# Attention, Fourier mixing and feed-forward on one core: seven block products in two more half batches, one exponential per score piece, and five PSUM banks in one ring

## The chip, the cores and the metric

The kernel runs on one core of a Trainium2 chip. A core has a matrix engine (TensorE, PE in the profile; its weight loads are the row PEld), a vector engine (VectorE, DVE), a scalar engine (ScalarE, ACT), a third one for elementwise work on SBUF (GpSimd, POOL) and a queue for transfers (SyncE, SP). Matrix products land in PSUM, which has eight banks of 128 x 512 fp32; DVE and ACT read them from there. The metric is the time of one execution on the device in microseconds, the median of several runs.

## What is computed

Eight batches of eight heads with 576 tokens and 64 dimensions each go through attention with a mask by blocks of 64. The heads are put together to 512 columns, mixed by a two-dimensional Fourier transform (the real part is added), and go through a normalisation and two layers with a relu between them:

```python
scores = scale * np.matmul(q, k.transpose(0, 1, 3, 2))
scores = np.where(block_i >= block_j, scores, -1000000000.0)
attn = np.exp(scores - np.max(scores, axis=-1, keepdims=True))
attn = attn / (np.sum(attn, axis=-1, keepdims=True) + 1e-09)
x = np.matmul(attn, v)                      # then 8 heads side by side: 576 x 512
X = np.fft.fft(np.fft.fft(x, axis=1), axis=2)
u = x + np.real(X)
un = (u - mu) / np.sqrt(var + 1e-06)
out = u + np.maximum(un @ w_ch1, 0.0) @ w_ch2   # 512 -> 2048 -> 512
```

## The kernel before, in words

All matrix products are made from fp16 pairs: a number is a high and a low half, and a product of two numbers is three matmuls (high by high, high by low, low by high).

**Attention** works head by head, 64 heads. For each head four pieces of scores are made for the row maxima (`max_part`, line 621), reduced by DVE into a tile `M`; `shift` (650) turns the maxima over on PE, ACT writes them to `mt`, and a transfer puts them into a row of the tile `lead`, so that the scores made next (`scores`, 680, four pieces too, from the tiles `rest` and `lead`) come out shifted already. ACT then takes the exponential of each piece twice from the PSUM bank, once into fp16 (`ph`) and once into fp32 (`p32`, shown as `p`), and POOL subtracts the two into the low half `pl`. `values` (708) multiplies them with the split values (`VH`, `VL`) into the bank `av`; DVE divides by the sums.

**The transform** of a batch (`fourier_steps`, 791) is folded and made in two stages on PE (`ps<-dft,fs` and `ps<-dft,zs` or `zc`). Of its second stage DVE makes `dif` and `add`, and POOL adds them to the tiles `X`, `U` and `u`, four operations for each of three pieces. What follows is the normalisation of 128 rows at a time (`norm`, 988: DVE statistics `st` and `ag`, a power on POOL, `un` on DVE), and `turn` (1002): PE turns it over, ACT and DVE split it into `uh` and `ul`.

**The feeds.** 256 rows at a time, a half batch, go through the two layers as one feed (`feed_steps`, 1036). There are 18 of them, and they are the bulk of PE's work. The first layer makes 16 blocks of 128 hidden columns (`h<-uh,W`, 256 columns per matmul); ACT and DVE split each pair of blocks into `gh` and `gl`; the second layer adds the products of these with the second weights (`acc<-W,gh`, 512 columns) into two banks `acc`. The feeds 15 to 17 (`SEVEN`, line 53) take the second layer by Strassen's seven products instead of eight (`seven`, 1135), 256 columns each, for each of 8 block pairs k: for this ACT writes the relu of the block in fp32 (`V`), POOL makes four sums of it (`x`, in `summed_up`, 1103), ACT and DVE split those (`ph`, `pl`). The sums of the weights (`combined`, 1405) are made after the last head, in the buffers that attention has left. Seven products need seven half banks for their sums: two `acc`, `av`, and one bank taken from `ps`.

**Order.** PE, DVE, ACT, POOL and SP each work strictly in the order in which the program was written. This order comes from a planner (1476 to 1532) that runs when the program is built: lanes of steps (attention, transform, weights) with assumed costs, and the feeds as filler between them. It books the assumed costs in a queue for each engine and gives PE the filler when no step of a lane is ready. Seven PSUM banks stand in three rings (`BANKS`, 51): `ps` three for attention and transform, `h` two for the first layer, `acc` two for the second; `av` has the eighth. Until the first feed begins all seven are lent to whoever asks; from then on steps get `ps` alone, and the feeds have `h` and `acc` to themselves.

## Time and profile before

| what | value |
|---|---|
| median of 3 runs | 1211.73 us (1210.74 to 1212.89) |
| profiled execution: time, span | 1207.94 us, 1206.1 us |
| TensorE clock granted, mean | 0.961 |
| busy, share of the span | PE 94%, PEld 70%, DVE 62%, ACT 50%, POOL 40% |
| instructions | PE 10338, DVE 1615, ACT 1338, POOL 630 |
| time of the DMA queues | q1 24.1%, q10 4.2%, q0 2.1% of 16 engines |

The profile is of one execution. It names tiles without their numbers, so `ps<-lead` stands for all maxima and half of the scores, `h<-uh,W` for the first layer, `acc<-W,gh` for the second. Nearly all instructions show the line 203, of a helper that keeps the order (229 and 232 for PE), so groups are told apart by tiles. A busy time of PE runs to the modelled end of each matmul; how fast matmuls follow each other is read from the starts.

### The profile page before, as it was taken

Reading aid. Unit: us, or ns where it says so; the run is one execution under the profiler, and the core shown is the slowest. Engines: PE = TensorE matmul, PEld = TensorE weight load, DVE = VectorE, ACT = ScalarE, POOL = GpSimd, SP = SyncE. Lnnn points to the kernel's source line nnn. Section 1 sums busy time; section 2 is a strip of 40 time slices with the busy share of each in tenths; the row PEclk is TensorE's granted clock in tenths of the full one; section 3 lists DMA queues with packets and bytes.
Section 4 is the critical chain, followed back from the end, with each engine's and each line's share of the span. In section 5 each row is a group of like instructions: output and inputs, shape, how many; then the busy total and the mean of one; then the engine's idle time right before and its main releaser. Section 6 shows DMA issues by size and latency. Waiting matters only on the chain.

```text
span 1206.1 us, 26181 instructions
## 1 busy us (share of the span) xinstructions
PE 1138.9 (94%) x10338; PEld 840.6 (70%) x10338; DVE 742.1 (62%) x1615; ACT 604.5 (50%) x1338; POOL 482.5 (40%) x630
## 2 busy tenths in 40 slices
PE   5767788999899999999999999999999999999998
PEld 4544475676677777777777777777677767788885
DVE  6877886666847673666647475757475657454421
ACT  5656667755565555536555346545554323233320
POOL 4552624534434434243442424353334333545420
PEclk9758789999799999999999999999999999999999
DMA  8785453333323342323325133413240010000000
GB/s 260 224 246 170 144 132 99 95 111 89 109 57 118 95 115 67 86 66 104 90 67 158 34 85 112 128 31 104 69 124 16 29 40 19 23 10 10 18 18 18
DMA packets 66128, 108.27 MB, mean 90 GB/s; under 512 B 9671, under 2 KB 36209, under 8 KB 66006
## 3 DMA queue, kind: packets, MB, share of 16 engines
q1 hardware_dynamic: 58662, 82.25, 24.1%
q10 hardware_dynamic: 4384, 16.78, 4.2%
q0 software_dynamic: 2960, 7.58, 2.1%
q8 instruction: 81, 1.33, 0.5%
q14 instruction: 41, 0.34, 0.1%
HBM read 58.50 MB, written 18.89 MB: 64 GB/s over the span
## 4 chain that ended last, share of the span: by engine, by line
PE 83%; DVE 5%; DMA 4%; POOL 3%; ACT 3%; issue 1%; SPq 0%; ACTq 0%; DVEq 0%; POOLq 0%
PE h L229 30%; PE acc L229 28%; PE ps L229 16%; PE av L229 8%; DMA lead<-mt 2%; DVE W L203 1%; POOL u L203 1%; PE ps L232 1%; DVE M L203 1%; POOL pl L203 1%; ACT p L203 1%; ACT ph L203 1%; ACT W L203 1%; DVE VL L203 1%; DMA lead<-rest 1%
## 5 line engine op out<-in xcount | busy, mean ns | idle before, releaser
L229 PE MATMUL h<-uh,W 128*128 128x256 f16 x2304 | 432.2, 274 | 0.2 <-DVE gl L203 0.2
L203 POOL TENSOR_TENSOR pl<-p,ph 128x288 f16<-128x288 f32 (+1 forms) x256 | 259.4, 1024 | 365.3 <-ACT p L203 337.0
L229 PEld LDWEIGHTS <-W 128*128 128x128 f16 x3456 | 332.7, 98 | 60.4 <-issue 1.3
L229 PE MATMUL h<-ul,W 128*128 128x256 f16 x1152 | 315.3, 274 | 0.0
L229 PE MATMUL acc<-W,gh 128*128 128x512 f16 (+1 forms) x1008 | 289.5, 370 | 0.0
L203 DVE TENSOR_REDUCE M<-ps 128x1 fp32r<-128x320 f32 (+3 forms) x293 | 131.3, 484 | 119.3 <-PE ps L229 118.8
L229 PE MATMUL acc<-W,gl 128*128 128x512 f16 (+1 forms) x504 | 186.2, 370 | 0.0
L229 PE MATMUL ps<-lead 73*128 73x288 f16 (+8 forms) x708 | 161.4, 291 | 15.4 <-DMA lead<-in_c_masks_dram 6.8
L203 ACT ACTIVATE ph<-ps 128x288 f16<-128x288 f32 (+1 forms) x235 | 119.5, 510 | 111.4 <-PE ps L229 110.6
L203 ACT ACTIVATE gh<-h 128x512 f16<-128x512 f32 x138 | 82.5, 598 | 166.6 <-PE h L229 161.6
L203 DVE SCALAR_TENSOR_TENSOR gl<-h,gh 128x512 f16<-128x512 f32 x138 | 94.7, 687 | 114.9 <-ACT gh L203 114.3
L229 PEld LDWEIGHTS <-ph 128*128 128x128 f16 x2112 | 133.1, 103 | 26.8 <-issue 4.6
L229 PEld LDWEIGHTS <-gh 128*128 128x128 f16 x1056 | 98.4, 99 | 67.8 <-issue 4.7
L229 PE MATMUL av<-VH,pl 128*128 128x65 f16 (+1 forms) x963 | 117.0, 201 | 8.4 <-POOL pl L203 6.5
L203 ACT ACTIVATE p<-ps 128x288 f32<-128x288 f32 (+1 forms) x235 | 119.0, 508 | 2.2 <-POOL pl L203 1.0
L229 PE MATMUL av<-VH,ph 128*128 128x65 f16 (+1 forms) x966 | 118.4, 203 | 0.7 <-ACT p L203 0.7
L229 PE MATMUL av<-VL,ph 128*128 128x64 f16 x960 | 116.7, 200 | 0.0
L229 PEld LDWEIGHTS <-pl 128*128 128x128 f16 x1056 | 103.5, 102 | 12.7 <-POOL pl L203 8.5
L229 PE MATMUL ps<-rest 128*128 128x320 f16 (+3 forms) x356 | 99.4, 292 | 1.0 <-DVE M L203 0.9
L229 PEld LDWEIGHTS <-lead 73*128 73x128 f16 (+1 forms) x744 | 66.7, 103 | 36.4 <-issue 8.1
L229 PEld LDWEIGHTS <-gl 128*128 128x128 f16 x528 | 51.5, 98 | 55.3 <-issue 0.5
L229 PEld LDWEIGHTS <-rest 128*128 128x128 f16 x372 | 38.8, 104 | 34.9 <-issue 15.3
(255 smaller groups left out, 1611.1 us busy)
## 6 DMA issues: line engine op xcount, KB each, us to landing
raw<-in_qk_dram SPq DMA_DIRECT2D x30, 576.0 KB
W<-in_moe_w_ch_dram ACTq DMA_DIRECT2D x14, 1024.0 KB
V<-in_v_dram SPq DMA_DIRECT2D x32, 320.0 KB
rest<-lead SPq DMA_DIRECT2D x64, 144.0 KB
rest<-rest SPq DMA_DIRECT2D x60, 144.0 KB
out_dram<-u SPq DMA_DIRECT2D x32, 256.0 KB
xd<-x SPq DMA_DIRECT2D x30, 256.0 KB
lead<-lead SPq DMA_DIRECT2D x60, 72.0 KB
```

The lines of the kernel that those rows point to most:

```text
L203: x = f(*args, **kw)
L229: return tc.keep_in_program_order(nc.tensor.matmul(*args, **kw))
L232: return tc.keep_in_program_order(nc.tensor.transpose(*args, **kw))
```

## The change

Five things are changed together.

1. `SEVEN` is 13 to 17 in place of 15 to 17: two more feeds take their second layer by seven products.
2. From head index 17 on (`ONCE`), `scores` takes one exponential per piece, into fp32, and ACT casts that copy to fp16 instead of reading the bank again. The bank is free after the first of the two.
3. Once feed 2 is done, the two `h` banks join the ring of `ps`: five banks, of which each step takes the one that has been free longest by the plan. A feed's first layer holds its bank from its first matmul to its last reader (`hold`, `drop`).
4. A new `pair_max` for two heads at once would begin at pair `GP`. `GP` is 32, and there are 32 pairs, so no step of it is ever made. What stays of it: four tiles `M` in place of two, six memsets of its constants on POOL at the very start, ahead of the transfers of the masks, three memsets of 64 columns, and split tiles that are shifted by 64 columns.
5. The planner leaves out single-bank steps that come later than a waiting step for two banks; there is no such step.

```diff
-SEVEN = range(15, 18)
+ONCE = 17
+SEVEN = range(13, 18)
+GP = 32
...
+    for i in range(2):
+        gpsimd.memset(MAIN[i], LEAST)
+        gpsimd.memset(MAIN[i][0:64, 0:1], 0.0)
+        gpsimd.memset(DIAG[i], LEAST)
     for i in range(HF):
         gpsimd.dma_start(LEAD[i][D:KS], c_masks)
...
+    def next_banks(n):
+        def first(x):
+            return (sorted(rings[x], key=lambda y: y[0]) if shared_out else rings[x])[:n]
+        return min(((x, first(x)) for x in lent if len(rings[x]) >= n), key=lambda x: max(y[0] for y in x[1]))
...
-        scalar.activation(ph[:, at:at + w], t[:, 0:w], AF.Exp, scale=0.125)
-        yield
+        if h < ONCE:
+            scalar.activation(ph[:, at:at + w], t[:, 0:w], AF.Exp, scale=0.125)
+            yield
         p32 = work.tile([P, 512], F32, name="p32", bufs=2)
         scalar.activation(p32[:, 0:w], t[:, 0:w], AF.Exp, scale=0.125)
         yield
+        if h >= ONCE:
+            scalar.copy(ph[:, at:at + w], p32[:, 0:w])
+            yield
         gpsimd.tensor_tensor(pl[:, at:at + w], p32[:, 0:w], ph[:, at:at + w], op=ALU.subtract)
...
     def max_lane():
-        for h in range(B * H):
+        for h in range(2 * GP):
...
+        for g in range(GP, B * H // 2):
+            for n in range(4):
+                yield Step(lambda n=n: pair_max(g, n), ...)
...
             if f % 2 == 0 and part == 0:
-                gs[f] = ps["h"].tile([P, 512], F32, name="h")
+                gs[f] = ps_tile() if me > 2 else own_tile()
...
     while True:
+        if not shared_out and ("F", 2) in done:
+            shared_out.append(True)
+            rings["ps"] += rings.pop("h")
```

The planner's inputs change, so the order changes on every engine. On PE the first 1744 matmuls are alike in the two orders; the one after them starts at 263.7 us of the trace; on DVE, ACT and POOL (but for the memsets) they part at about the same place. From there attention runs further ahead: in the new order the last head's values stand at a place with 107 us less PE work before it.

First place, the exponentials, on ACT: pieces 3 and 4 of one head, which `ps_3913` and its neighbour hold (`p` is the fp32 copy, `bs` the transform's). Before:

```order
L203 ACTIVATE ph_3911<-ps_3913 128x512
L203 ACTIVATE p_3967<-ps_3913 128x512
L203 ACTIVATE ph_3933<-ps_3935 128x512
L203 ACTIVATE p_3988<-ps_3935 128x512
L203 COPY bs<-ps_3977 128x258
```

The same place on ACT in the new order:

```order
L211 ACTIVATE p_3974<-ps_3913 128x512
L211 CAST ph_3911<-p_3974 128x512
L211 ACTIVATE p_3993<-ps_3928 128x512
L211 CAST ph_3926<-p_3993 128x512
L211 COPY bs<-h_3986 128x258
```

The count stays the same; `ph` comes second now, and only one instruction of each pair reads the bank.

Second place, DVE between the two normalised halves (`un`) of feed 3 and their split (`ul`), at 311 to 317 us of the trace of before. `M` rows are attention's maxima, `vacc` and `pw` a scale of attention. Before:

```order
L203 TENSOR_SCALAR un_4190<-u_3220,ag_4151 128x512
L203 TENSOR_SCALAR un_4204<-u_3220,ag_4171 128x512
L203 TENSOR_REDUCE M_0_94<-ps0_4181 128x1
L203 TENSOR_REDUCE M_0_94<-ps1_4194 128x1
L203 COPY vacc_4126<-ps0_4230 128x3
L203 TENSOR_SCALAR pw_4234<-vacc_4126 128x2
L203 SCALAR_TENSOR_TENSOR vacc_4126<-pw_4234 128x1 x2
L203 TENSOR_SCALAR pw_4234<-vacc_4126 128x1
L203 TENSOR_SCALAR vacc_4126<-pw_4234 128x1
L203 TENSOR_TENSOR ul_4254<-ps1_4255,uh_4253 128x4x128
L203 TENSOR_TENSOR ul_4254<-ps2_4261,uh_4253 128x4x128
```

The same place on DVE now:

```order
L211 TENSOR_SCALAR un_4241<-u_3238,ag_4197 128x512
L211 TENSOR_REDUCE M_2_99<-ps1_4191 128x1
L211 TENSOR_REDUCE M_2_99<-h0_4193 128x1
L211 TENSOR_REDUCE M_2_99<-ps0_4243 128x1
L211 TENSOR_SCALAR M_2_99<-M_2_99 128x1
L211 TENSOR_SCALAR un_4320<-u_3238,ag_4204 128x512
L211 TENSOR_SCALAR DEN_0_105<-av_4213,vacc_3294 128x5
L211 RECIPROCAL rec_4334<-DEN_0_105 128x5
L211 TENSOR_TENSOR x_4332<-av_4213,rec_4334 128x5x64
L211 TENSOR_TENSOR ul_4255<-ps1_4256,uh_4254 128x4x128
L211 COPY vacc_4154<-ps2_4325 128x3
```

Maxima and one head's division stand between the two halves now, and the second `ul` follows nine rows below the last of these.

Third place, POOL where the last batch's transform meets the feeds by seven products. `X`, `U` and `u<-u,dif` or `add` with 257 or 255 columns are the transform's, `x` the sums of seven products. Before, at 1038 to 1045 us, in feed 15:

```order
L203 TENSOR_TENSOR X_14755<-X_14755,dif 33x257
L203 TENSOR_TENSOR X_14755<-X_14755,add 33x255
L203 TENSOR_TENSOR U_14754<-U_14754,add 32x257
L203 TENSOR_TENSOR U_14754<-U_14754,dif 32x255
L203 TENSOR_TENSOR x<-V 128x128 x2
L203 TENSOR_TENSOR x<-x,V 128x128
L203 TENSOR_TENSOR x<-V,x 128x128
L203 TENSOR_TENSOR u<-u,dif 128x257
L203 TENSOR_TENSOR u<-u,add 128x255
```

And on POOL now, between the feeds 14 and 15 (the first two rows are the end of feed 14):

```order
L211 TENSOR_TENSOR u<-u,dif 128x256
L211 TENSOR_TENSOR u<-u,add 128x256 x2
L211 TENSOR_TENSOR X_15044<-X_15044,dif 33x257
L211 TENSOR_TENSOR X_15044<-X_15044,add 33x255
L211 TENSOR_TENSOR U_15043<-U_15043,add 32x257
L211 TENSOR_TENSOR U_15043<-U_15043,dif 32x255
L211 TENSOR_TENSOR u<-u,dif 128x257
L211 TENSOR_TENSOR u<-u,add 128x255
L211 TENSOR_TENSOR u<-u,add 128x257
L211 TENSOR_TENSOR u<-u,dif 128x255
L211 TENSOR_TENSOR x<-V 128x128 x2
L211 TENSOR_TENSOR x<-x,V 128x128
```

The sums for the first block pair of a feed by seven products stand behind ten rows of the transform and of the feed before, where they stood behind four. The transform of the batch before that one now meets the start of feed 13 in the same way; before, it met attention.

More of the change, by code (lines that the diff above doesn't have):

```diff
@@ L160 @@
     key: object = None
-    bank: bool = False
+    bank: int = 0
+    hold: object = None
+    drop: object = None
     need: tuple = ()
@@ L280, in split @@
         if g == GF:
-            return tuple(stage[i].rearrange("p c d -> p (c d)").bitcast(F16)[:, 0:2 * S] for i in range(2))
+            return tuple(stage[i].rearrange("p c d -> p (c d)").bitcast(F16)[:, 0:(64, 0)[i] + 2 * S] for i in range(2))
         return half_tiles(g % 2)[2:4]
-    M = [const.tile([P, 6], F32R, name=f"M_{i}") for i in range(2)]
+    M = [const.tile([P, 6], F32R, name=f"M_{i}") for i in range(4)]
+    MAIN, DIAG = ([const.tile([P, 5], F32, name=f"{x}_{i}") for i in range(2)] for x in ("MAIN", "DIAG"))
     DEN = [const.tile([P, 5], F32, name=f"DEN_{i}") for i in range(2)]
@@ L320, in ready @@
         if step.bank:
-            return max(r, min(rings[x][0] for x in lent))
+            return max(r, *(x[0] for x in next_banks(step.bank)[1]))
         if step.place > H and not step.cost:
@@ L357, in issue @@
                 x.forget(now)
-        free = None
+        free = []
         starts = []
@@ L378, in issue @@
         if step.bank:
-            current = min(lent, key=lambda x: rings[x][0])
-            rings[current] = rings[current][1:] + [t if free is None else free]
+            ring, got = next_banks(step.bank)
+            rings[ring] = [x for x in rings[ring] if not any(x is y for y in got)] + got
+            for n, x in enumerate(got):
+                x[0] = float("inf") if step.hold else free[min(n, len(free) - 1)] if free else t
+            if step.hold:
+                held[step.hold] = got[0]
+            given[:] = got
+        if step.drop in held:
+            held.pop(step.drop)[0] = t
         parts = step.emit()
@@ L1191, in both_steps @@
                     after = (("t", me, 0), ("t", me, 1)) + ((("g", me, k - 2),) if k > 1 else ())
-                yield Step(lambda part=part: both(k, part), 0.654, (), after, ("h", me, k) if last else None)
+                yield Step(
+                    lambda part=part: both(k, part), 0.654, (), after, ("h", me, k) if last else None, 0 if part else 1,
+                    hold=None if part else ("h", me, k),
+                )
         def split_steps(k):
@@ L1211, in feed_steps @@
             if not seventh:
-                seventh.append(turned.pop(0))
-                taken.append(rings["ps"].pop(0))
+                one = min(rings["ps"], key=lambda x: x[0])
+                rings["ps"] = [x for x in rings["ps"] if x is not one]
+                seventh.append(one[1:])
             nk = NF // 2
@@ L1485, in tile_attn_fourier_ffn @@
         ]
+        claim = min((heads[i].place for i in able if heads[i].bank == 2 and max(done[x] for x in heads[i].after) <= now), default=None)
+        if claim is not None:
+            able = [i for i in able if heads[i].bank != 1 or heads[i].place <= claim]
         until = [ready(heads[i]) for i in able] + ([ready(filler)] if filler is not None and may(filler) else [])
@@ L1525, in tile_attn_fourier_ffn @@
             if len(lent) > 1:
-                now = max(now, ready(filler), *rings["h"], *rings["acc"])
+                now = max(now, ready(filler), *(x[0] for x in rings["h"] + rings["acc"]))
                 lent = ["ps"]
```

95 lines of the change are left out of this document (68 added, 27 removed).

## The prediction

> **What bounds the kernel now.** I read the page first, for the engine that is busy and for when it is not.
>
> ```profile
> span 1206.1 us, 26181 instructions
> PE 1138.9 (94%) x10338; PEld 840.6 (70%) x10338; DVE 742.1 (62%) x1615; ACT 604.5 (50%) x1338; POOL 482.5 (40%) x630
> PE   5767788999899999999999999999999999999998
> PEclk9758789999799999999999999999999999999999
> ```
>
> PE is the only engine near its limit, and its gaps lie in the first quarter. The stretches of the trace say where exactly (columns: length, busy time of PE, PEld, DVE, ACT and POOL with instructions, clock granted, DMA share, GB/s).
>
> ```profile
> 0.00:264.00 264.00, 209.62 (x1747) 145.31 (x1748) 199.81 (x422) 174.48 (x383) 119.24 (x136) 0.85 0.56 169
> 264.00:292.00 28.00, 28.00 (x266) 20.23 (x265) 16.41 (x38) 15.46 (x39) 8.39 (x9) 1.00 0.06 17
> 292.00:318.00 26.00, 19.02 (x179) 14.23 (x178) 22.45 (x53) 13.93 (x34) 16.29 (x23) 0.74 0.60 170
> 318.00:400.00 82.00, 82.00 (x855) 60.02 (x853) 53.33 (x119) 47.56 (x110) 33.60 (x38) 1.00 0.28 83
> 400.00:700.00 300.00, 300.00 (x2875) 220.59 (x2873) 180.05 (x429) 150.11 (x343) 119.39 (x148) 1.00 0.32 88
> 700.00:1040.00 340.00, 340.00 (x3060) 246.32 (x3059) 207.34 (x449) 153.41 (x347) 125.58 (x152) 1.00 0.24 68
> 1040.00:1060.00 20.00, 18.36 (x166) 16.12 (x165) 11.96 (x25) 7.42 (x15) 16.90 (x33) 1.00 0.03 7
> 1060.00:1080.00 20.00, 20.00 (x186) 17.99 (x184) 6.49 (x11) 6.74 (x12) 6.94 (x16) 1.00 0.01 1
> ```
>
> Four stages follow. Up to 264 us PE waits a good deal, but its order there is not changed. From 292 to 318 us it idles 7 of 26 us: feed 2 is over, feed 3 waits for the transform of its batch, and DVE is busy 22.45 of 26. From 318 to 1040 us PE never rests, at full clock: only fewer or shorter matmuls can shorten this. At 1040 to 1060 it loses 1.64 us where the last transform meets feed 15. So the change can win by PE work, and win or lose at 292 and wherever a transform meets seven products.
>
> **The seven products.** The chain that ended last shows a feed with the plain second layer, per pair of blocks:
>
> ```profile
> 949.30 2.59 PE acc L229 x12
> 951.89 2.62 PE h L229 x24
> 954.51 2.59 PE acc L229 x12
> ```
>
> and, as further lines of that chain, one with seven products:
>
> ```profile
> 1060.35 2.62 PE h L229 x24
> 1062.96 0.66 PE acc L229 x6
> ...
> 1065.26 2.62 PE h L229 x24
> ```
>
> A plain pair takes 954.51 - 949.30 = 5.21 us, of which 12 matmuls of 512 columns are 2.59, 216 ns each. With seven products it is 1065.26 - 1060.35 = 4.91: 21 matmuls of 256 columns in 2.29 us, 109 ns each, about half as long for half the columns. The gain is 0.30 us a pair, 2.4 a feed with 8 pairs, **-4.8 us** for two feeds, all of it on PE where nothing hides it. The 16 pairs bring ACT, POOL and DVE work; beside a steady feed of that kind PE has 20.00 busy of 20 (row 1060:1080), so it is hidden there. The Trainium skill, "TensorE: Matmul & The Clock Gate", section "Back-to-back issue gap", gives a lower sustained spacing for streams with weight loads, about 131 ns at 512 columns and 81 at 128. An estimate by that page, with 98 ns between them for 256 columns, would be 96 x 131 = 12.6 us against 168 x 98 = 16.5, a loss of 3.9 us a feed. The rows above speak against it: 216 and 109 ns.
>
> **The start.** Six memsets now stand on POOL ahead of the masks' transfers, and the chain that ended last runs through these transfers:
>
> ```profile
> 2.06 4.65 DMA lead<-in_c_masks_dram
> ```
>
> POOL's timeline has memsets of this kind:
>
> ```profile
> 0.25 0.10 POOL L1561 MEMSET const-float32-0.0<- 128x1 f32 x1 [0.25 <-issue]
> 0.28 0.10 POOL L1561 MEMSET const-float32-1.0<- 128x1 f32 x1
> ```
>
> They follow each other by 0.03 us and take 0.10 each, so six delay the masks by 0.2 to 0.6 us, with nothing above them to hide it; a wait further on that is not for the masks may still swallow part. I take **+0.2**, the value by spacing. The three other memsets stand behind the work that frees their tiles, 0.1 us on an idle POOL: nothing.
>
> **One exponential.** Groups by form at 320 to 940 us (instructions, busy time, mean ns, idle time before):
>
> ```profile
> L203 ACT ACTIVATE ph<-ps 128x512 f16<-128x512 f32 x84 | 50.7, 605 | 19.9 <-PE ps L229 19.3
> L203 ACT ACTIVATE p<-ps 128x512 f32<-128x512 f32 x84 | 50.4, 602 | 0.8 <-POOL pl L203 0.6
> ```
>
> and the nearest row to a cast from SBUF, from the groups at 1030 to 1206 us:
>
> ```profile
> L203 ACT CAST ph<-x 128x512 f16<-128x512 f32 x24 | 14.8, 618 | 37.5 <-POOL x L203 37.5
> ```
>
> 618 ns against 605: ACT pays 0.01 us a piece, with half its time idle. `pl` waits for the second of the two in either order, `values` for `pl`, and the bank is free 0.6 us earlier. Priced alone, at 318 to 1040 us, where PE is full, it is **0**; a bank that frees earlier is worth something only where PE waits for banks.
>
> **Five banks, and attention ahead.** From 318 us on, PE is full before; the new order is worth nothing there unless it brings waits. Counted from the orders with the trace's spacing, the least PE work between a head's `shift` and its first scores is 4.0 us now and 4.3 before, and between a head's scores and its `values` 4.2 and 3.6. So the covers are of one size, and I take **+0.4** for the tighter transfers, between 0 and 3. The maxima, casts and DVE work of a head come 20% more densely while attention runs, which DVE at 180 of 300 us can carry.
>
> **The stage at 292 us.** What PE waits for there:
>
> ```profile
> PE ps L229 <- DVE M L203: 3.5, 3, 2.3
> ```
>
> and DVE's groups in this stage:
>
> ```profile
> L203 DVE TENSOR_REDUCE M<-ps 128x2 fp32r<-128x128 f32 (+4 forms) x14 | 6.0, 467 | 1.1 <-PE ps L229 1.1
> L203 DVE BATCH_NORM_STATS2 st<-u 128x6 f32<-128x512 f32 x3 | 2.0, 675 | 0.0
> L203 DVE TENSOR_TENSOR dif<-ps,bs 128x258 f32<-128x258 f32 (+1 forms) x3 | 1.3, 418 | 0.6 <-POOL U L203 0.6
> L203 DVE TENSOR_TENSOR x<-av,rec 128x320 f32<-128x320 f32 x1 | 0.5, 492 | 0.0
> ```
>
> Feed 3 begins when DVE has made its second `ul`. From the end of feed 2 to there, DVE's new order has three more maxima (3 x 0.467 = 1.4), one more division of a head (0.5 for `x`, 0.4 for its two small ones) and one more statistics (0.7 and 0.2 for the small row), and one `dif` and `add` less (0.8): about 2.4 us more on the engine that is busy 22.45 of 26. In return PE has done more by then: 14.0 us of work in place of 12.8 stand in the stage, and 2.1 us more before it. So feed 3 starts up to 2.4 us later with 3.3 us more done: **-0.9**. If DVE's extra falls into its 3.5 idle us, it is -3.3; if the low clock (0.74) also slows the 3.3 us of extra work to half speed, +2.4.
>
> **Transforms that meet seven products.** How it goes before: POOL's timeline has the transform's sums,
>
> ```profile
> 1042.77 1.41 POOL L203 TENSOR_TENSOR u<-u,add 128x255 f32<-128x255 f32 x2
> 1046.09 1.86 POOL L203 TENSOR_TENSOR u<-u,add 128x255 f32<-128x255 f32 x2
> ```
>
> and PE's waits of that time are
>
> ```profile
> 1047.42 0.28 PE L229 MATMUL av<-raw,pl 128*128 128x256 f16 x1 [0.89 <-DVE pl L203]
> ...
> 1053.47 0.66 PE L232 MATMUL ps<-ident,un 128*128 128x128 f32 x4 [0.74 <-DVE un L203]
> ```
>
> The sums `x` of seven products stand behind the transform's on POOL, then ACT and DVE split them, then PE gets them: 0.89 + 0.74 = 1.63 us, the idle time of 1040:1060. The transform of batch 6, hidden in attention before, now meets the start of feed 13 with the same rows on POOL: **+1.6**. The last transform stands between the feeds 14 and 15, with three sums of feed 14 ahead of it (0.7 us each by the rows above) and 5.6 us of PE work from its last matmul to the turn of feed 15, where 7.5 stood; in return that turn no longer waits for the last four `u`, 2.8 us. These about cancel: **+0.4**, between -1 and +3.
>
> **The sum.** -4.8 + 0.2 + 0 + 0.4 - 0.9 + 1.6 + 0.4 = -3.1 us, against the profiled execution's 1207.94 us (span 1206.1 and 1.84 around it): 1204.8. The median of the runs shown, 1211.73, is 3.8 above that execution; the terms are differences, so I take them from the median: **1208.6**.
>
> **Rivals.** A measurement of this kernel tells 0.2%, 2.4 us, from no change.
>
> *Waits eat the gain.* If both meetings cost 3 us each instead of 2.0 together, and the stage at 292 gives nothing: -4.8 + 0.2 + 0.4 + 6 = +1.8 at most, -0.5 with half of that; 1211.2. For it: PE has less work to put in between now that attention is over early. Against: after 1060 us the same feeds run without a gap. Chance 0.25.
>
> *The stage at 292 closes.* With five banks for attention, PE may make maxima and scores while DVE is late, and keep its clock: of the 7 us idle, 5 go: -4.8 + 0.2 + 2 - 5 = -7.6, 1204.1. Against: the row of waits names DVE, not banks. Chance 0.10.
>
> *The stage at 292 grows, and it ends slower.* DVE is the bound there. If the nine rows between the two `ul` wait for PE, whose matmuls stand behind a wait for DVE, the two go in turns, at the low clock. Feed 3 then starts 10 us later than I take it (the stage once more, by its 7 us of idle time and 3 at half speed): -3.1 + 10 = +6.9, 1218.6; from 5.5 us on it ends slower. Against: PE has 14 us of work there. Chance 0.10.
>
> *DVE and POOL lock each other out.* One `pl<-x,ph` on DVE's timeline shows 1.19 us while POOL's 1.86 above ran; the mean of its group at 1030 to 1206 us, below it, is 0.713:
>
> ```profile
> 1046.17 1.19 DVE L203 TENSOR_TENSOR pl<-x,ph 128x512 f16<-128x512 f32 x1
> ```
>
> ```profile
> L203 DVE TENSOR_TENSOR pl<-x,ph 128x512 f16<-128x512 f32 x24 | 17.1, 713 | 29.1 <-ACT ph L203 29.1
> ```
>
> With 16 more such instructions, each late by 0.48 us and none hidden, 7.7 us come on top: +4.6, 1216.3. Against: the mean says that most are not late, and the row 1060:1080 that PE does not see it. Chance 0.05. The Trainium skill, "SBUF — State Buffer", section "Who interferes with whom", says that a DVE instruction with two SBUF inputs and a POOL instruction that reads SBUF exclude each other for their whole length, which is this mechanism; the 1.19 us agrees.
>
> *The change does not do what it says.* For two heads' maxima at once this is certain (no step is made); for the rest the order shows it done.
>
> **How the numbers follow.** The forecast has 0.50, from 1204.5 to 1209.3. Faster by over 0.2%: 0.50 + 0.10 = 0.60, less 0.03 for its upper edge, 0.57. Same: 0.25 + 0.03 = 0.28. Slower: 0.10 + 0.05 = 0.15. The range goes from 1203 (the stage closes) to 1214 (all meetings at their upper bounds).
>
> **What would show it.** PE's last work should come 3 us earlier, the feeds 13 and 14 should have groups of 21 between those of 24, and 318 to 860 us should have no gap. A wait of PE for DVE `pl` or `un` should show at the start of the feeds 13 and 15, 1 to 3 us in sum each. The stretch from feed 2 to feed 3 should be 26 to 29 us long. I am wrong if that stretch is under 20 or over 35, or if PE has gaps while attention runs beside the feeds.

## The result, and the profile after

The changed kernel takes 1215.63 us (median of 11 runs, 1213.91 to 1222.28), the kernel before 1208.17 beside it (11 runs, 1207.33 to 1212.89): a ratio of 1.0063 with a 95% interval of 1.0045 to 1.0080. It is slower by 5 to 10 us; forecast was 3.1 us faster, and the range ended at 1214.0. The forecast of 1208.6 us was counted from a median of 1211.73 for before, 3.6 above the 1208.17 beside this result, so the two times lie only 7.0 us apart where the differences lie 10.6 apart. The profiled execution of it took 1219.95 us, 12.0 more than that of before and 4.3 more than its own median, so terms read from it are at the high end. Single executions that took over 1.5% longer than the fastest of their kernel (one of after_two_exp, one of cover_four_late, one of before in a later group) are left out of all ratios and medians below.

From the page after, the span, the totals and the two rows of PE in 40 slices:

```profile
span 1218.2 us, 26794 instructions
PE 1138.9 (93%) x10482; PEld 855.1 (70%) x10482; DVE 762.6 (63%) x1643; ACT 641.4 (53%) x1372; POOL 521.2 (43%) x709
PE   5667788999799999999999999999999999999998
PEclk9757789999799999999999999999999999999999
```

At this grain the two profiles can hardly be told apart. So I cut both at marks of the program: the last matmul up to which the orders agree (number 1744), the first of feed 3, of feed 13 and of feed 16. These are the first three stretches after that common part, of before (length, then busy time of PE, PEld, DVE, ACT, POOL with instructions, clock, DMA share, GB/s):

```profile
263.70:317.90 54.20, 47.22 (x447) 34.65 (x445) 38.76 (x90) 29.59 (x71) 24.78 (x32) 0.87 0.32 91
317.90:941.20 623.30, 623.30 (x6047) 456.26 (x6046) 380.98 (x886) 321.97 (x741) 248.09 (x304) 1.00 0.30 85
941.20:1080.40 139.20, 137.56 (x1091) 105.24 (x1090) 78.69 (x145) 43.63 (x87) 54.41 (x83) 1.00 0.07 24
```

and the same of after:

```profile
266.40:325.80 59.40, 50.25 (x504) 36.63 (x502) 43.75 (x99) 35.99 (x81) 29.02 (x38) 0.89 0.30 84
325.80:950.50 624.70, 619.42 (x5999) 451.19 (x5999) 402.68 (x916) 344.14 (x748) 258.38 (x303) 1.00 0.30 85
950.50:1092.60 142.10, 138.39 (x1224) 122.74 (x1223) 71.84 (x134) 52.24 (x102) 76.51 (x148) 0.99 0.07 23
```

The middle row of each is the news: 623.30 busy of 623.30 before, 619.42 of 624.70 after. The stretch that "never rests" now rests 5.28 us. The first stretch idles 9.15 us in place of 6.98, the last 3.71 in place of 1.64.

Idle time leaves out what a wait costs besides: matmuls that start again at a low clock, and short gaps that the tail of the matmul before covers. So in what follows I use **lost time**: the time from the start of one matmul to the start of another, less the spacing that each matmul between them has where PE is full (the median from start to start for its form, from 350 us of the trace of before on: 109 ns at 256 columns, 216 at 512). The sum of the spacings is PE's pure work: 1124.8 us before, 1119.9 after. In us, by stretch:

| kernel | PE work | to matmul 1744 | to feed 3 | feed 3 to 13 | feeds 13 to 15 | rest |
|---|---|---|---|---|---|---|
| before | 1124.8 | 55.4 | 13.2 | -1.0 | 2.2 | 0.6 |
| after | 1119.9 | 57.6 | 15.1 | 6.6 | 7.1 | 0.3 |

(A loss below zero is a few matmuls that follow each other faster than the median.) The first matmul starts 0.46 us later (below). 0.46 + 2.2 + 1.9 + 7.6 + 4.9 - 0.3 - 4.9 = 11.9: the 12.0 us are accounted for. What remains is to find which of it comes from what.

**The attention stage.** What PE waits for from 325 to 935 us, a list that is empty for the same stretch of before:

```profile
PE acc L244 <- DVE gl L211: 1.1, 1, 1.1
PE ps L244 <- DVE M L211: 1.1, 2, 0.7
PE ps L244 <- DMA lead<-rest: 0.9, 1, 0.9
PE ps L244 <- DVE vacc L211: 0.8, 1, 0.8
...
PE ps L244 <- ACT p L211: 0.3, 1, 0.3
```

No large wait, but a handful of small ones on DVE, ACT and transfers. In lost time, ten matmuls from feed 3 to feed 13 start over 0.25 us later than their spacing has it, 6.9 us in sum. Five of them (3.2 us) follow a read by DVE or ACT that has nothing to do with their operands, so I take it that they wait for the bank; three of these (1.7 us) are first layers of feeds. Three (2.9 us) wait for something of their own: the maxima, the transfer `lead<-rest`, and a feed's second layer for its own `gl` (1.3 us). For two (0.8 us) the trace names no reason. One of the first kind, on PE's timeline:

```profile
543.58 0.27 PE L244 MATMUL ps<-uh,W 128*128 128x256 f16 x1 [0.68 <-DVE M L211]
```

and on DVE's:

```profile
541.45 0.68 DVE L211 BATCH_NORM_STATS2 st<-left 128x6 f32<-128x512 f32 x1
542.16 0.18 DVE L211 BATCH_NORM_AGGREGATE ag<-st 128x2 f32<-128x6 f32 x1
542.26 0.67 DVE L211 BATCH_NORM_STATS2 st<-left 128x6 f32<-128x512 f32 x1
542.97 0.18 DVE L211 BATCH_NORM_AGGREGATE ag<-st 128x2 f32<-128x6 f32 x1
543.07 0.99 DVE L211 TENSOR_REDUCE M<-ps 128x1 fp32r<-128x320 f32 x2
```

`ps<-uh,W` is the feed, the work that PE always has in hand. Its bank belonged before to the feeds alone; now it comes from attention, whose maximum is still to be read by DVE, and DVE has the statistics of a row block in front of it. The work that was to hide attention's waits has in part become one that waits.

**Where transforms meet seven products.** The chain that ended last, at the start of feed 13, and PE's and POOL's timelines between the feeds 14 and 15:

```profile
958.24 1.24 POOL x L211 x3
960.02 2.75 POOL u L211 x4
963.55 0.60 DVE gl L211
964.15 1.11 DVE pl L211
965.59 0.66 PE acc L244 x6
```

```profile
1046.99 0.28 PE L244 MATMUL h<-dft,ZT 128*128 128x258 f32 x1
1049.09 1.11 PE L244 MATMUL h<-dft,zs 128*128 128x258 f32 x6 [1.82 <-ACT bs L211]
```

```profile
1046.69 1.41 POOL L211 TENSOR_TENSOR u<-u,add 128x256 f32<-128x256 f32 x2 [0.38 <-DVE u L211]
1048.06 0.72 POOL L211 TENSOR_TENSOR X<-X,dif 33x257 f32<-33x257 f32 x1
1048.74 0.72 POOL L211 TENSOR_TENSOR X<-X,add 33x255 f32<-33x255 f32 x1
```

The first is as forecast: the sums `x` of the products and the transform's `u` take turns on POOL, and feed 13 loses 1.39 us (0.07 before). The second is one step back: `bs` of the transform waits on ACT for DVE's `add`, `add` for POOL, and PE stands still in the middle of the transform. The feeds 14 and 15 lose 0.82 and 4.91 us (0.02 and 2.12 before).

**The products themselves** do what was forecast. Pairs of feed 13 on the chain that ended last:

```profile
977.50 2.62 PE ps L244 x24
980.12 0.66 PE acc L244 x6
...
982.41 2.62 PE ps L244 x24
```

982.41 - 977.50 = 4.91 us a pair, where a plain pair takes 5.21.

### The profile page after: what moved, and what is told of

It is laid out like the page before. It is cut to its first block, busy times and chain, and to the rows that moved or that the text cites. A ratio compares the mean times of both kernels' runs of the same rounds, so it can differ in the third digit from the quotient of the medians.

```text
span 1218.2 us, 26794 instructions
## 1 busy us (share of the span) xinstructions
PE 1138.9 (93%) x10482; PEld 855.1 (70%) x10482; DVE 762.6 (63%) x1643; ACT 641.4 (53%) x1372; POOL 521.2 (43%) x709
## 4 chain that ended last, share of the span: by engine, by line
PE 76%; DVE 8%; POOL 5%; DMA 5%; issue 3%; ACT 3%; SPq 1%; ACTq 0%; DVEq 0%; POOLq 0%
PE ps L244 25%; PE acc L244 25%; PE h L244 17%; PE av L244 8%; DMA lead<-mt 2%; POOL u L211 2%; DVE W L211 2%; DVE M L211 1%; POOL pl L211 1%; DMA lead<-rest 1%; PE ps L247 1%; DMA u<-in_moe_w_ch_dram 1%; SPq L211 1%; POOL U L211 1%; POOL X L211 0%
## 5 line engine op out<-in xcount | busy, mean ns | idle before, releaser
L244 PE MATMUL ps<-uh,W 128*128 128x256 f16 x1296 | 240.1, 274 | 1.4 <-DVE M L211 0.7
L244 PE MATMUL h<-uh,W 128*128 128x256 f16 x1008 | 187.7, 277 | 0.4 <-DVE vacc L211 0.2
L244 PE MATMUL ps<-ul,W 128*128 128x256 f16 x648 | 177.1, 273 | 0.0
L244 PE MATMUL h<-ul,W 128*128 128x256 f16 x504 | 139.4, 277 | 0.0
L244 PE MATMUL ps<-lead 73*128 73x288 f16 (+11 forms) x463 | 111.0, 300 | 20.0 <-DMA lead<-in_c_masks_dram 7.3
L211 DVE TENSOR_REDUCE M<-ps 128x1 fp32r<-128x192 f32 (+4 forms) x187 | 85.5, 491 | 49.7 <-PE ps L244 49.5
L211 ACT ACTIVATE p<-ps 128x288 f32<-128x288 f32 (+1 forms) x161 | 80.4, 500 | 40.3 <-PE ps L244 34.3
L211 ACT CAST ph<-p 128x512 f16<-128x512 f32 (+1 forms) x188 | 98.3, 523 | 5.1
L211 ACT ACTIVATE gh<-ps 128x512 f16<-128x512 f32 x81 | 48.0, 593 | 86.3 <-PE ps L244 83.5
L211 DVE SCALAR_TENSOR_TENSOR gl<-ps,gh 128x512 f16<-128x512 f32 x81 | 55.5, 685 | 55.7 <-ACT gh L211 55.0
```

Source lines behind the costliest of these rows:

```text
L211: x = f(*args, **kw)
L244: return tc.keep_in_program_order(nc.tensor.matmul(*args, **kw))
```

## The experiments

The theory after this comparison: PE's work did fall by 4.9 us, and three losses ate it: attention put further ahead with shared banks (about 7.6 us in the profiled pair), transforms beside seven products (4.9), and the stage at 292 us (1.9). The rivals: the cast is behind the attention stage's loss; the memsets are behind the later start; the crowded order is harmless and only the meetings cost. Beside the first four kernels, before took 1209.09 us (23 runs), beside the next four 1209.06 (29). Each group of kernels ran on another chip beside runs of before, so kernels of different groups are compared by their ratios to it.

### One part at a time

Three kernels make one part each, one takes the memsets from the changed kernel.

`seven_alone`, from before:

```diff
-SEVEN = range(15, 18)
+SEVEN = range(13, 18)
```

> The kernel before with one edit: seven products also in the feeds 13 and 14 (SEVEN from 13). Its order is that of before up to those feeds, and only the last transform meets them. Theory 'crowded order' (shared banks and attention pulled ahead cost the time, the feeds' gain is real): PE has 4.8 us less work, the last meeting costs about 1 us more; 1208.2 - 4.8 + 1 = 1204.4, ratio 0.997. Theory 'meeting' (the waits where transform and seven products meet eat the gain): 1208 to 1210, ratio 1.000 or above, with 4 us or more of new PE gaps between 940 and 1110 us.

1238.05 us, a ratio of 1.0242 (1.0223 to 1.0261): neither theory had 29 us. The stretch of the feeds 13 to 15, the wait in it, and what ACT makes there:

```profile
943.80:1110.00 166.20, 139.72 (x1234) 121.03 (x1233) 100.06 (x173) 62.93 (x120) 93.44 (x153) 0.95 0.07 20
```

```profile
967.69 0.37 PE L229 MATMUL ps<-raw,gh 128*128 128x256 f16 x1 [10.82 <-ACT raw L203]
```

```profile
966.10 0.62 ACT L203 CAST raw<-p 128x512 f16<-128x512 f32 x1 [2.75 <-DVE p L203]
```

`raw` here is no raw input any more. The second layer's summed weights are put into the tiles that attention leaves, and are made after its last head:

```python
            yield Step(
                lambda: combined(k), 0.0, ("X3.1", "A1.25", "G2.35"),
                (("V", B * H - 1, 4),) + ((("TT", k - 1),) if k else ()), ("TT", k),
            )
```

They take DVE, ACT and POOL from 966 to 1013 us here (46.7), and from 864 to 937 in the changed kernel (73). With attention's last head at 869 us of PE work and feed 13 at 867 there is no time for them, and feed 13 waits for one pair of weights after the other. I had not seen this in the forecast: the two more feeds of seven products can only be had because the shared banks pull attention ahead (its last head stands at 765 us of PE work in the changed kernel). The parts of this change aren't independent.

`once_alone`, from before:

```diff
+ONCE = 17
...
-        scalar.activation(ph[:, at:at + w], t[:, 0:w], AF.Exp, scale=0.125)
-        yield
+        if h < ONCE:
+            scalar.activation(ph[:, at:at + w], t[:, 0:w], AF.Exp, scale=0.125)
+            yield
...
+        if h >= ONCE:
+            scalar.copy(ph[:, at:at + w], p32[:, 0:w])
+            yield
...
```

The planner's list of assumed costs for a piece is changed to match.

> The kernel before with the one exponential per piece from head 17 on, nothing else. Theory 'crowded order' and theory 'meeting': 1208 +- 2, ratio within 0.998 to 1.002. Theory 'cast' (the cast holds ph, pl and the buffer of p longer, and PE waits for them in the attention stage): 1212 or more, ratio 1.003 or above, with PE gaps of 3 us or more at 320 to 940 us and PE's waits there naming ACT p or POOL pl.

1210.13 us, 1.0016 (1.0000 to 1.0031): at most a small loss. From feed 3 to feed 13 it loses 2.9 us (before -1.0). PE's waits of that stretch:

```profile
PE acc L231 <- DVE gl L205: 2.7, 1, 2.7
PE av L231 <- POOL pl L205: 0.8, 1, 0.8
```

The largest is one wait for `gl` in the second layer of feed 12, and `pl` comes to 0.8 us; beside the last transform the kernel wins 1.7 back. So the theory 'cast' falls as the main cause.

`banks_alone`, from after:

```diff
-ONCE = 17
+ONCE = 64
-SEVEN = range(13, 18)
+SEVEN = range(15, 18)
```

> The changed kernel with two exponentials and seven products as before, so the five shared banks (and the order that follows: attention further ahead of the feeds), the memsets at the start and the reordered small steps alone. Theory 'crowded order': 1208.2 + 3.6 (the stage from 292 us) + 5 to 6 (small PE gaps at 400 to 800 us) = 1217, ratio 1.007, PE busy 97 to 99 of 100 in the stretches from 400 to 700 us. Theory 'meeting' or 'cast': 1208 +- 2, no PE gaps at 400 to 700 us.

1212.18 us, 1.0029 (1.0013 to 1.0044): a loss of 1.6 to 5.3 us, less than the 'crowded order' has it, more than nothing. The attention stage, with once_alone's below:

```profile
319.20:947.40 628.20, 623.51 (x6041) 455.69 (x6042) 412.57 (x927) 326.03 (x754) 262.05 (x310) 1.00 0.31 86
```

```profile
316.20:945.30 629.10, 625.34 (x6096) 457.15 (x6095) 385.50 (x888) 342.56 (x745) 253.73 (x304) 1.00 0.31 85
```

PE idles 4.69 us in the one and 3.76 in the other.

`after_no_memsets`, from after:

```diff
-        gpsimd.memset(MAIN[i], LEAST)
-        gpsimd.memset(MAIN[i][0:64, 0:1], 0.0)
-        gpsimd.memset(DIAG[i], LEAST)
```

> The changed kernel without the six memsets on POOL ahead of the masks' transfers (their tiles are read by nothing). Theory 'start' (the 2.7 us by which the changed kernel was late at its 1744th matmul come from the memsets): 1215.6 - 2.5 = 1213. As the prediction has it: 0.2 us, 1215.4. If the lateness is only the scatter between executions: 1215.6.

1218.56 us, 1.0070 (1.0051 to 1.0088): nothing is won. In the trace of after, the memsets do move the masks' transfer from 2.06 to 2.54 us, as forecast (0.2 to 0.6):

```profile
2.05 0.27 POOL L211 MEMSET MAIN<- 128x5 f32 x2
2.27 0.10 POOL L211 MEMSET DIAG<- 128x5 f32 x1
...
2.54 1.06 POOL L211 DMA_DIRECT2D lead<-in_c_masks_dram  x2
```

But up to matmul 1744 this kernel without memsets lost 61.1 us, more than any other; over the 20 profiled executions of this study that part, whose order never changes, lost 51.0 to 61.1 us, on the mean 55.3 in the 16 with memsets and 57.3 in the four without. The lateness of 2.7 us that I had seen at matmul 1744 is the scatter between executions.

### One part undone, and two repairs

`after_seven_late` (SEVEN from 15 again) and `after_two_exp` (ONCE = 64), from after:

> The changed kernel with seven products as before (from feed 15 only); one exponential and five shared banks stay. Theory 'meeting' (the feeds 13 to 15 of the changed kernel lose 1.4, 0.8 and 4.9 us against their spacing, 2.2 in all before, so the 4.8 us of saved PE work are lost again): about the time of the changed kernel, 1215 to 1217. Theory 'the products pay' (the loss lies elsewhere, and the two feeds save 4.8 less 2): 2.8 us slower than the changed kernel, 1218.5.

1216.31 us, 1.0072 (1.0046 to 1.0098): the time of the changed kernel. The feeds 13 to 15 lose 0.15 us here in place of 7.1, with 4.9 us more PE work. The gain of the seven products is real, and what they lose by meeting transforms is as large.

> The changed kernel with two exponentials per piece; five shared banks and seven products from feed 13 stay. Theory 'meeting': the time of the kernel with the banks alone (1.0029) plus nothing, 1211 to 1213, ratio 1.003. Theory 'together only' (one exponential and shared banks cost 6 us in the attention stage together, 1 to 2 each alone): also 1211 to 1213, with PE's loss from feed 3 to feed 11 at 1 to 2 us in place of 6.2. If the products pay by themselves: 1209.

1213.01 us, 1.0041 (1.0025 to 1.0057), nearer to banks_alone (1.0029) than to the changed kernel (1.0063), though the intervals overlap on both sides. But its attention stage lost 7.1 us in the profiled execution, not 1 to 2: 'together only' is not what the trace shows. Its order there is that of banks_alone, which lost 4.6, so one order scatters by some 2.5 us between executions. (The order of the changed kernel lost 6.6, 5.4, 6.0 and 4.7 us in its four executions.)

`after_cover`, from after: a step of attention goes ahead of a ready feed only when the planner has held it ready for longer, 0.8 us in place of 0.3. I call this time the cover.

```diff
-        sure = now - ((LATE if seventh else MARGIN) if feed and ready(filler) <= now else 0.0)
+        sure = now - ((LATE if seventh else 0.8 if shared_out else MARGIN) if feed and ready(filler) <= now else 0.0)
```

> The changed kernel, with a step of attention put ahead of a feed only when the planner holds it ready for 0.8 us in place of 0.3, once the banks are shared. Attention is as far ahead as before the edit (its last head at 771 us of PE work, 765 in the changed kernel). Theory 'thin cover' (PE's small gaps in the attention stage are steps that the planner holds ready and that are late by up to 1 us): the 6.2 us lost from feed 3 to feed 11 fall to 2 or less, 1211 to 1212, 4 us under the changed kernel. Theory 'too much work on DVE and ACT' (the readers are late whatever the order is): the gaps move and stay 5 us or more, 1215 to 1217.

1209.72 us, 1.0005 (0.9991 to 1.0019), where the changed kernel has 1.0063, with attention as far ahead as there:

```profile
323.60:938.40 614.80, 614.54 (x5985) 448.54 (x5985) 404.37 (x914) 343.35 (x746) 259.95 (x303) 1.00 0.31 87
```

PE is busy 614.54 of 614.80, and the loss from feed 3 to feed 13 is -1.5 us, as before. DVE has 404 us of work in that stretch, as in the changed kernel (403), so 'too much work on DVE and ACT' falls: the loss of the attention stage is the order's. The four kernels of the next section have the same order of PE up to feed 13 and lose -1.3 to -0.1 us there.

`after_late_transform`, from after:

```diff
-LATE = 0.3
+LATE = 2.0
```

> The changed kernel, with a step of a transform put ahead of a feed of seven products only when the planner holds it ready for 2.0 us in place of 0.3. The order is the same up to the third last feeds. Theory 'meeting, by order' (PE waits 2.0 us for the transform's bs, which ACT makes after POOL's sums, and 0.7 for un; the planner puts these steps too early): of 4.9 us lost from feed 15 on, 2 to 3 go, 1212.5 to 1213.5. Theory 'meeting, by work' (POOL and DVE cannot do both in time): the wait moves to the next feed, 1215 to 1217.

1213.87 us, 1.0038 (1.0022 to 1.0055), 2.5 thousandths under the changed kernel, but the intervals overlap; the feeds 13 to 15 lose 4.1 us in place of 7.1 in the profiled executions. So part of the meeting's loss seems to be order, and part stays.

### Both repairs, and the meeting avoided

Four kernels on the base of after_cover, before at 1208.75 us beside them (35 runs). Their edits to it:

```diff
 cover_seven_late
-SEVEN = range(13, 18)
+SEVEN = range(15, 18)
 cover_late_transform
-LATE = 0.3
+LATE = 2.0
 cover_four_feeds
-SEVEN = range(13, 18)
+SEVEN = (13, 15, 16, 17)
 cover_four_late
-SEVEN = range(13, 18)
+SEVEN = (13, 15, 16, 17)
-LATE = 0.3
+LATE = 2.0
```

> The kernel after_cover (steps of attention only when ready for 0.8 us), with seven products as before, from feed 15. Theory 'meeting': against after_cover it has 4.8 us more PE work and loses 6 us less where the transforms meet the products (6.5 us from feed 13 on there, about 0.4 in after_seven_late), so 1208.5, ratio 0.9995. If the products paid by themselves: 4.8 - 2 slower than after_cover, 1212.5.

1208.92 us, 1.0009 (0.9994 to 1.0024): as 'meeting' has it. Two more feeds of seven products are worth nothing (after_cover: 1.0005) while they meet the transform.

> The kernel after_cover, with steps of a transform beside seven products only when ready for 2.0 us. If the two edits work on different losses, their gains add: after_cover's 1209.7 less the 2 us that the late transform gave alone, 1207.7, ratio 0.9988. If the second loss was partly the same: 1209 to 1210.

1207.57 us, 0.9990 (0.9978 to 1.0002): the value that adding the two gains gives, though its interval overlaps that of after_cover (1.0005). The feeds 13 to 15 lose 4.4 us in place of 6.3.

> The kernel after_cover, with seven products in the feeds 13, 15, 16 and 17; feed 14, in which the last transform runs, keeps the plain second layer. Theory 'meeting' (the loss is a transform and seven products side by side): PE has 2.4 us less work than before, and loses less than 1 us from feed 13 on, where before lost 2.6: 1209 - 2.4 - 2 = 1204.6, ratio 0.9965, faster than before. Theory 'crowding' (DVE and POOL have that work in any case, and the wait moves to the start of feed 15): 1207 to 1209.

1207.26 us, 0.9984 (0.9969 to 0.9998): the only kernel of these experiments whose interval lies below before's time, and that barely, by 0.2 to 3.7 us. Its feeds 13 to 15:

```profile
942.50:1082.00 139.50, 139.50 (x1166) 116.80 (x1165) 65.32 (x122) 44.27 (x87) 59.52 (x113) 1.00 0.07 23
```

No gap is left, so the wait has not moved to feed 15 and 'crowding' falls, since DVE and POOL have the same transform to make; the time alone, 1207.26, lies in the range of 'crowding' and would not have told. The step from before is smaller than the 4.4 us expected; the stretch up to feed 3 loses 2.1 us more than before in it, which I had left out of that sum.

> The kernel cover_four_feeds, with steps of a transform beside seven products only when ready for 2.0 us; the last transform ends at 977 us of PE work there in place of 960, so it reaches into feed 15 of seven products (from 954). Theory 'meeting': 1 to 2 us slower than cover_four_feeds. Theory 'by order': the same within 0.5 us, or faster.

1207.31 us, 1.0004 (0.9991 to 1.0017). The ratio is 2.0 thousandths over that of cover_four_feeds, but the intervals overlap and the medians are the same (1207.31 and 1207.26), so the time decides nothing. In the trace the feeds 13 to 15 lose 2.7 us in place of 0.3, but only 0.7 of it in feed 15, into which the transform reaches; 1.9 are lost in feed 13, where the products of the last block pair wait for ACT's `ph`. So 'meeting' does not get its 1 to 2 us in feed 15 here, and the two theories are not told apart.

### How much cover, and the sharing undone

Whether 0.8 us was a measure or a lucky order was tried with five more covers in the same line of after (0.5, 0.6, 0.72, 0.78, 0.82). Before stood at 1211.77 us beside the first two and 1210.75 beside the other three.

> The changed kernel with a cover of 0.5 us in place of 0.3 for steps of attention, once the banks are shared. Theory 'thin cover' (waits of up to 1 us are cut by the 0.2 us that the cover grew, each): of the 6.6 us that PE loses from feed 3 to feed 13, 2 to 4 stay; 1212 to 1213.5. Theory 'luck': any value from -1 to 7 us of loss, without order by cover.

1218.38 us, 1.0055 (1.0036 to 1.0074); loss from feed 3 to feed 13: 7.1 us.

> The same with a cover of 0.6 us. Theory 'thin cover': 0.5 to 2.5 us of loss from feed 3 to feed 13, less than with 0.5; 1211 to 1212. Theory 'luck': any value from -1 to 7 us.

1218.90 us, 1.0058 (1.0040 to 1.0076); 5.3 us. Both miss what 'thin cover' had: it doesn't work step by step.

> The changed kernel with a cover of 0.72 us; attention's last head at 773 us of PE work. Theory 'threshold' (a cover of some 0.7 us is longer than the single instructions of DVE and ACT that made steps late): less than 1 us of loss from feed 3 to feed 13, ratio 1.0005 +- 0.0015. Theory 'luck of the order': 2 us or more of loss in at least one of the three orders with 0.72, 0.78 and 0.82.

1214.78 us, 1.0021 (1.0002 to 1.0040); 3.3 us. Nearly all of it is one wait for the transfer of a head's maxima:

```profile
PE h L244 <- DMA lead<-mt: 3.5, 1, 3.5
```

> The same with 0.78 us; attention's last head at 796 us of PE work. Theory 'threshold': less than 1 us of loss, ratio 1.0005 +- 0.0015. Theory 'luck of the order': 2 us or more in at least one of the three.

1213.75 us, 1.0015 (1.0001 to 1.0030); -0.9 us.

> The same with 0.82 us; attention's last head at 797 us of PE work. Theory 'threshold': less than 1 us of loss, ratio 1.0005 +- 0.0015. Theory 'luck of the order': 2 us or more in at least one of the three.

1213.58 us, 1.0020 (1.0008 to 1.0032); 2.3 us.

So a plain 'threshold' falls as well (two of three lost over 2 us), and so does plain 'luck': the covers of 0.3 to 0.6 us lose 4.7 to 7.1 us and stand at 1.0055 to 1.0063, those of 0.72 to 0.82 lose -1.5 to 3.3 and stand at 1.0005 to 1.0021. (With 0.78 and 0.82 attention is also less far ahead, its last head at 796 and 797 us of PE work in place of 765; with 0.72 and 0.8 it is at 773 and 771.) A longer cover takes most of the loss away; what is left differs from order to order, and which of the single waits an order will meet stays open.

`after_no_sharing`, from after, gives the feeds their own two banks back:

```diff
-                gs[f] = ps_tile() if me > 2 else own_tile()
+                gs[f] = own_tile()
...
-                gs[k] = ps_tile()
+                gs[k] = own_tile()
...
-        if not shared_out and ("F", 2) in done:
-            shared_out.append(True)
-            rings["ps"] += rings.pop("h")
```

> The changed kernel with the feeds' two banks kept apart from attention's three, so that one exponential and the seven products from feed 13 stay, and attention's last head stands at 850 us of PE work (765 in the changed kernel, 869 in seven_alone). The weights of the seven products are summed after the last head, over 46 to 73 us in the traces. Theory 'sums first': feed 13 (from 869) again waits for these sums, less than the 30 us of seven_alone by the 19 us that attention ends earlier: 10 to 15 us of loss, 1217 to 1224. Theory 'the sums are not the reason': 1206 to 1210.

1229.26 us, 1.0146 (1.0108 to 1.0184). Feed 13 loses 21.7 us here (30.5 in seven_alone): the direction is that of 'sums first', and the size more than I had for it, because 19 us of earlier PE work bring the sums forward by less: ACT makes the first of them 29 us earlier than in seven_alone (937 and 966 us), but the last only 9 us earlier (1003 and 1013), and the loss falls by 8.8. Sharing the banks is worth about 8 thousandths, 10 us, in this change: 1.0146 stands against 1.0063.

From feed 3 to feed 13 this kernel loses 4.9 us, though no bank is shared in it. Its longest wait there is the one that once_alone has in feed 12:

```profile
PE acc L244 <- DVE gl L211: 2.7, 1, 2.7
```

The lost times of these kernels, without the five covers above:

| kernel | PE work | to matmul 1744 | to feed 3 | feed 3 to 13 | feeds 13 to 15 | rest |
|---|---|---|---|---|---|---|
| seven_alone | 1119.9 | 58.0 | 12.8 | -0.8 | 34.2 | 0.6 |
| once_alone | 1124.8 | 54.8 | 12.4 | 2.9 | 0.5 | 0.6 |
| banks_alone | 1124.8 | 53.7 | 13.3 | 4.6 | 0.1 | 0.3 |
| after_no_memsets | 1119.9 | 61.1 | 15.2 | 5.4 | 7.3 | 0.3 |
| after_seven_late | 1124.8 | 55.7 | 14.9 | 6.0 | 0.2 | 0.3 |
| after_two_exp | 1119.9 | 58.9 | 13.4 | 7.1 | 5.8 | 0.3 |
| after_cover | 1119.9 | 55.0 | 14.1 | -1.5 | 6.3 | 0.3 |
| after_late_transform | 1119.9 | 56.6 | 15.6 | 4.7 | 4.1 | 0.7 |
| cover_seven_late | 1124.8 | 52.6 | 14.6 | -1.3 | 0.2 | 0.3 |
| cover_late_transform | 1119.9 | 56.2 | 15.3 | -0.7 | 4.4 | 0.1 |
| cover_four_feeds | 1122.4 | 57.0 | 15.3 | -0.1 | 0.3 | 0.3 |
| cover_four_late | 1122.4 | 51.0 | 15.1 | -0.7 | 2.7 | 0.3 |
| after_no_sharing | 1119.9 | 53.6 | 12.3 | 4.9 | 25.3 | 0.6 |

Up to feed 13 several of these kernels have one and the same order of matmuls on PE, so the column "feed 3 to 13" shows what an order costs and how it scatters. The order of before lost -1.0 and -0.8 us (seven_alone), that of the changed kernel 4.7 to 6.6 in four executions, that of banks_alone 4.6 and 7.1 (after_two_exp), that of once_alone 2.9 and 4.9 (after_no_sharing), that of after_cover -1.5 to -0.1 in five. All but the last were made with a cover of 0.3 us, and of those only before's loses nothing. Shared banks are not needed for such a loss, since once_alone and after_no_sharing share none. Whether before's order is free of waits by luck, no run here tests.

## Why the prediction was wrong

The sign was wrong, and the sum missed by some 10 us: forecast -3.1, measured 5 to 10 slower. Step by step:

- **Seven products, -4.8.** Right: 4.91 us a pair in feed 13, PE's work 4.9 us less. The estimate by the Trainium skill's "TensorE: Matmul & The Clock Gate", section "Back-to-back issue gap" (a loss of 3.9 us a feed), is not borne out by any of these pairs.
- **The start, +0.2.** Right in its bounds (0.48 us in the trace), and lost in the scatter of that stretch.
- **One exponential, 0.** The price of the cast was right, 615 ns where I had 618:

```profile
L211 ACT CAST ph<-p 128x512 f16<-128x512 f32 x86 | 52.9, 615 | 2.2
```

  Taken alone the part costs 0 to 3.7 us by its interval, and its order lost 2.9 and 4.9 us from feed 3 to feed 13. I held it for nothing because PE was full at 318 to 1040 us, and did not ask what its new order would bring there.
- **Five banks and attention ahead, +0.4 (0 to 3).** This step failed, and it is the largest: 4.7 to 6.6 us of loss in the four executions of that order, where before gained 1.0. I had argued that the least cover for a head's own steps, between `shift` and scores and between scores and `values`, is of one size in both orders. That may be so, and is beside the point. About half of what waits (3.2 of 6.9 us in the profiled execution) is not those steps but the next user of a shared bank, the feed among them, behind DVE's or ACT's read of it; and for that I had counted no cover at all. The other half waits for maxima, for the transfer `lead<-rest` and for a feed's own `gl`; of these the sum had only transfers, at 0.4 us. "DVE at 180 of 300 us can carry" it was a share of busy time, where a delay of 1 us at one instruction decides. The five executions with after_cover's order show that the order and not the work is the reason; sharing banks is one way to such an order, and once_alone's order is another. The prediction did name this sign for its being wrong: "if PE has gaps while attention runs beside the feeds".
- **The stage at 292 us, -0.9.** Failed in sign. The six kernels (before among them) in which one exponential, shared banks or both are missing lose 12.3 to 13.4 us up to feed 3, the 14 that have both lose 14.1 to 15.6. That is 2 us more on the mean: inside the range that I had (-3.3 to +2.4), at its far end. The stretch from feed 2 to feed 3 is 29.2 us long (last matmul of feed 2 at 296.6, feed 3 at 325.8), at the upper edge of the 26 to 29 that I had. What PE waits for there has changed from `M` to `add` and the transfer of the maxima:

```profile
304.51 0.28 PE L244 MATMUL ps<-rest 128*128 128x288 f16 x1 [1.70 <-DVE add L211]
308.32 0.40 PE L244 MATMUL ps<-lead 73*128 73x288 f16 x1 [3.53 <-DMA lead<-mt]
```

  These are the attention steps that I had counted as work that PE would have done by then; they waited themselves, on DVE's `add` in front of the scores' bank and on a transfer.
- **Batch 6 at feed 13, +1.6.** Right in place, mechanism and size: 1.3 us more than before.
- **The last transform between the feeds 14 and 15, +0.4 (-1 to +3).** The step failed in size: +3.6 us (0.82 and 4.91 in the feeds 14 and 15, 0.02 and 2.12 before). I had it cancel against waits at the turn; the wait came earlier, inside the transform (`bs` behind `add` behind POOL), 1.82 us and behind it a low clock (some 1.7 us of the 3.6), which does not come in every execution, as the last section shows. cover_four_feeds, which keeps that feed plain, loses 0.3 in all three feeds.
- **The parts taken as separate terms.** seven_alone and after_no_sharing show that they are not: the products need the early end of attention. The sum was still the right one for the whole change, as its order has the sums done in time.

Of the rivals, "waits eat the gain" has the mechanism, with the waits in the meetings; the larger part of them was in the attention stage, where it had none. (Its -0.5 us does not come out of its own terms: half of 6 us gives -1.2, and 1210.5 in place of 1211.2.) The lock of DVE and POOL was no part of it that these runs can price.

## What to carry to other kernels

A stretch in which an engine is busy 100% proves that the present order has cover enough, and says nothing on another order; price a new order by every wait that it may meet: who reads each shared buffer last and how late that reader may come, also for the filler work where it takes buffers from the same ring, and how late the filler's own operands may come. When parts of a change use the same freed space, look for the step on which the other parts wait (here the weights' sums after the last head) before adding up terms. And where a gain is eaten, first try to move the meeting: keeping one feed plain and asking 0.5 us more of cover turned +0.6% into -0.2%, which is just clear of no change.

## What the runs showed of the hardware

**The clock after a short wait.** PE's 1.82 us of waiting at 1047 us were followed by a stretch at half the full clock, though PE had been full for long. In the 20 traces every change of the granted clock lies on a grid of 3.41 us, which runs through the whole trace. The step of the grid with that wait and the next one, in after:

```profile
1046.37:1049.78 3.41, 1.59 (x13) 1.39 (x12) 0.99 (x3) 0.37 (x1) 3.09 (x5) 1.00 0.00 0
1049.78:1053.19 3.41, 3.41 (x18) 2.58 (x17) 0.82 (x3) 1.36 (x3) 2.87 (x5) 0.50 0.32 97
```

A step at a clock of 0.50 costs 1.7 us of PE work on top of the wait (0.5 x 3.41). Nine executions have this wait for `bs`, 1.82 to 1.84 us long. In four (after, after_no_memsets, after_two_exp, after_cover) it lies in one step of the grid, and the next step has the low clock. In the five others (the covers of 0.5 to 0.82) it lies across two steps, and the clock stays at 1.00, as in after_cover_06:

```profile
1041.24:1044.65 3.41, 1.94 (x18) 1.65 (x15) 2.04 (x6) 0.06 (x1) 2.76 (x4) 1.00 0.00 0
1044.65:1048.06 3.41, 2.31 (x18) 1.87 (x18) 0.76 (x2) 0.71 (x3) 2.87 (x6) 1.00 0.12 29
```

So what one wait costs depends on where in the grid it falls, and that differs between executions. From 330 us to the last matmul, 14 steps at full clock have 1.8 us or more of idle PE in the 20 traces; 12 of them are followed by the low clock (the exceptions have 1.86 us in after_cover_072 and 2.02 in once_alone), and no step with less is. The Trainium skill, "TensorE: Matmul & The Clock Gate", section "What's actually happening", has the low clock come after an idle window of about 3.4 us, in a grid that runs freely. The grid agrees with the traces, and the wholly idle window does not: here 1.82 us of idle time in it were enough.

**A small DVE instruction held for POOL's length.** In the attention stage of after, on DVE and on POOL:

```profile
550.31 0.17 DVE L211 TENSOR_SCALAR pw<-vacc 128x2 int32<-128x2 int32 x1
...
666.34 0.83 DVE L211 TENSOR_SCALAR pw<-vacc 128x2 int32<-128x2 int32 x1
```

```profile
665.28 1.85 POOL L211 TENSOR_TENSOR pl<-p,ph 128x288 f16<-128x288 f32 x2
```

The second `pw` is the same instruction on two columns, and ends (667.17) when POOL's two `pl` end (667.13). The Trainium skill, "SBUF — State Buffer", section "Who interferes with whom", says that DVE's `tensor_scalar` can take the ports that it shares with POOL, and that of the two the later one is then shut out for the whole instruction of the other; the trace agrees. Five of the 63 `pw` take 0.47 us or more in either trace, 4.1 us in sum over their usual 0.17 before and 3.3 after; the longest, 2.36 us at 299 us of before, stands on the chain that ended last. In after_cover there are ten of them (6.6 us) and PE loses nothing from feed 3 to feed 13, so such holds alone do not make the loss of the attention stage.
